# First layer by token halves, the second half a period behind it, and a rewritten prologue and first period

## The chip, the core and the metric

The kernel runs on one core of a Trainium2 chip. The metric is the device time of one execution in microseconds (us). Three runs of the kernel before gave 299.66 to 300.46, median 300.08.

## What is computed

For each of 8 batches ("blocks" below) and 8 heads, q, k and v are 576 x 64. Landmarks are means over 18 neighbouring tokens, 32 for q and 32 for k. Then

```
A  = softmax(q  @ k_lm.T / 8)      # 576 x 32
Bm = softmax(q_lm @ k_lm.T / 8)    # 32 x 32
C  = softmax(q_lm @ k.T / 8)       # 32 x 576
Z  = Bm.T / (norm1(Bm) * norminf(Bm) + 1e-6)
for _ in range(6): Z = 2 * Z - Z @ Bm @ Z
attn = A @ Z @ C @ v               # 576 x 64 per head
```

The heads are put side by side into x (4608 x 512), and two dense layers follow: h = x @ w_in (512 x 2048), g = h * sigmoid(h), out = g @ w_out (2048 x 512). Inputs and output are float32; the products run in bf16.

## The kernel before

Eight heads are held as two groups of four, with 4 x 32 landmark rows on the 128 partitions. x is never formed. The kernel folds Z, C, v and w_in into one matrix per block: z_mm gives zwT, and four m_units multiply it by w_in, 512 columns each, into mb (256 x 2048 as two halves of 128 rows). A unit is eight products of 64x32 tiles into two PSUM buffers, copied out by VectorE (L460) and ScalarE (L461). The first layer is then AT (A transposed, 256 x 576) against mb.

The program is written out by hand in the order in which each engine is to work. A prologue (L515 to L587) does all the attention of block 0. After it comes a loop of one "period" per block b, of 16 steps s. Step s of period b does one of the first layer's 16 slices of 128 columns for all 576 tokens (l1_mm, L469, four "hps" products into a two-bank PSUM tile; l1_act, L479, Silu by ScalarE into gT). Around it are laid the attention of block b + 1 and the second layer of block b - 1: l2_mm(n) (L489) issues the next n of its "ops" products. Sixteen ops fill one output tile of 128 tokens in the pool pso, which has one buffer; then ScalarE copies it to ost (L505) and SyncE stores it. An even block has four such tiles and an odd one five, since the 64 tokens left over of an even block are put at the front of the odd one (l1_tail, L484, on GpSimd). The lists EVEN and ODD (L510) say how many ops each step issues: 80 in an even period, 64 in an odd one. The tiles of block b are put into the queue at the end of period b (L733), so none is issued in period 0, and the five of block 7 follow the last period.

The attention of block b + 1, in order: landmarks (lmn; for blocks 0 and 1 by 18 "lmp" products per plane with the identity on TensorE, L151; for the others by GpSimd sums, L164); bdiag (L198) spreads their transposes into block-diagonal weights bd by four VectorE transposes of 32 partitions, and a fifth gives lmk; b_scores, b_max, b_exp, b_norm (Bm); f_mm, b_scale and f_out make the start of the iteration; six rounds of ns_mm and ns_step (L279 to L293) carry F = Z Bm and X as 128 + 32 columns ("fx"; the first 128 hold four heads' 32x32 blocks on the diagonal); c_scores, c_max, c_exp (C); c_transpose and c_out for blocks 0 and 1, a transposing DMA for the others; w_mm, w_out (C @ v); x_out, z_mm, z_out; a_scores in three parts, a_max, a_shift, a_exp, a_norm (A; the last product on GpSimd, L427), and AT by a_transpose and a_out (blocks 0 and 1) or by DMA.

In a period with d = 0 bdiag is in step 0, scores in 1 and 2, with the Exp table loaded for them and the Silu table after them (table, L119, a small ScalarE activation behind a table load), the rounds in steps 3 to 9, z_mm in 10 and the m_units in 11 to 14. In period 0, d = 4: steps 0 to 3 make the landmarks of block 1, the rest is four steps later, and three m_units of block 1 stand behind step 15 (L729). Loads go out from GpSimd's queue (load_qk, load_v, and the weights at L107 and L112). PSUM's eight banks are: psh, two tiles of two banks (hps and scp); pso, one; psa, three, for all else.

## Time and profile before

| | us |
|---|---|
| median of three runs | 300.08 |
| the profiled execution, its own time | 300.44 |
| its span in the profile | 298.7 |
| first hps product (end of the prologue) | 32.38 |
| first hps product of block 1 (end of period 0) | 65.94 |
| last run of ops products begins | 276.71 |
| PE busy in the span | 266.3 (89%) |

PE is TensorE's products, PEld its weight loads, DVE VectorE, ACT ScalarE, POOL GpSimd, SP SyncE. A row of the timeline has the start, the duration, the engine, the line of the program, the operation, what is written from what, and how many instructions are merged into it; a bracket gives the idle time before it and what ended that. Products overlap, so busy time is not a sum of separate times. PEclk in the slices is the granted TensorE clock in tenths.

### The profile page before, as it was taken

The page shows a single profiled execution, that of the slowest core. Times are in us where ns is not written, and L with a number is a line of the kernel's source. Part 1 is how long each engine was busy: PE and PEld are TensorE (multiplying, and loading weights), DVE is VectorE, ACT ScalarE, POOL GpSimd, SP SyncE. Part 2 cuts the span into 40 slices and gives each one's busy share as a digit, 9 for nine tenths or more (in the row PEclk, how much of TensorE's full clock was granted, in tenths as well). Part 3 has the DMA queues.
Part 4 walks back from the last instruction along what each step waited for, and adds up shares of the span by engine and source line. Part 5 has one row for each costly group of instructions (what it writes and reads, how often), then busy time and mean ns, then how long its engine had stood idle before and what let it go on. Part 6 is the DMA issues. An engine that isn't in the chain of part 4 may idle for free.

```text
span 298.7 us, 5888 instructions
## 1 busy us (share of the span) xinstructions
PE 266.3 (89%) x2305; PEld 150.7 (50%) x2340; DVE 165.8 (55%) x407; ACT 174.2 (58%) x337; POOL 118.2 (40%) x141
## 2 busy tenths in 40 slices
PE   1766886769999999999999999999999999999994
PEld 1543564525554555455645554465555554455441
DVE  4885689786668565746695567475757523000000
ACT  1225288356757874669567855686669556445211
POOL 7234321893199119740794079204940300100000
PEclk9999999787999999999999999999999999999999
DMA  6999999507673946629597939131903131110111
GB/s 111 208 211 207 207 210 202 70 15 134 115 102 90 188 95 96 130 44 183 100 148 114 170 40 151 46 79 53 175 35 72 34 97 37 38 68 35 72 70 70
DMA packets 36252, 32.30 MB, mean 108 GB/s; under 512 B 18816, under 2 KB 27008, under 8 KB 36224
## 3 DMA queue, kind: packets, MB, share of 16 engines
q0 software_dynamic: 13568, 18.35, 37.5%
q1 hardware_dynamic: 22656, 13.57, 20.0%
q8 instruction: 18, 0.29, 0.5%
q14 instruction: 10, 0.08, 0.1%
HBM read 36.70 MB, written 9.44 MB: 154 GB/s over the span
## 4 chain that ended last, share of the span: by engine, by line
PE 79%; DVE 9%; ACT 4%; issue 3%; DMA 2%; POOL 1%; ACTq 0%; POOLq 0%
PE ops L71 43%; PE hps L71 19%; PE sa L71 5%; PE mp L71 4%; ACT ost L505 3%; PE scp L71 2%; DMA nat<-in_q_dram 2%; DVE qkT L148 2%; PE fi L71 2%; PE wp L71 1%; PE lmp L71 1%; DVE cmx L306 1%; DVE arec L425 1%; DVE fx L289 1%; DVE fx L274 1%
## 5 line engine op out<-in xcount | busy, mean ns | idle before, releaser
L71 PE MATMUL ops<-w_out_sb,gT 128*128 128x512 bf16 x541 | 141.1, 382 | 5.3 <-ACT ost L505 2.0
L481 ACT ACTIVATE gT<-hps 128x576 bf16<-128x576 f32 x128 | 82.4, 651 | 69.0 <-PE hps L71 68.6
L71 PE MATMUL hps<-AT,mb 128*128 128x288 bf16 x512 | 85.3, 293 | 0.3 <-ACT gT L481 0.2
L71 PEld LDWEIGHTS <-gT 128*128 128x128 bf16 x576 | 52.2, 98 | 54.2 <-issue 11.3
L71 PEld LDWEIGHTS <-mb 128*128 128x128 bf16 x512 | 48.4, 100 | 25.8 <-issue 2.8
L427 POOL TENSOR_TENSOR an<-ex,arec 128x512 bf16<-128x512 bf16 (+1 forms) x24 | 21.4, 906 | 86.9 <-ACT gT L481 43.8
L148 DVE STREAM_TRANSPOSE qkT<-nat 128x576 f32<-128x576 f32 x32 | 39.7, 1240 | 1.6 <-DMA nat<-in_k_dram 1.2
L505 ACT COPY ost<-ops 128x512 f32<-128x512 f32 x36 | 21.1, 586 | 23.9 <-PE ops L71 22.1
L289 DVE SCALAR_TENSOR_TENSOR fx<-fx,fi 128x320 bf16<-128x320 bf16 (+1 forms) x48 | 20.7, 431 | 23.1 <-PE fi L71 23.0
L460 DVE CAST mb<-mp 128x512 bf16<-128x512 f32 x32 | 22.0, 688 | 14.4 <-PE mp L71 14.1
L170 POOL TENSOR_TENSOR lma<-nat 128x1152 f32<-128x1152 bf16 x12 | 28.6, 2380 | 0.0
L461 ACT CAST mb<-mp 128x512 bf16<-128x512 f32 x32 | 18.7, 583 | 4.6 <-PE mp L71 4.6
L121 ACT ACT_TABLE_LOAD x16 | 20.5, 1283 | 1.1 <-PEq L749 0.8
L71 PE MATMUL fi<-fx 128*128 128x160 bf16 (+1 forms) x96 | 14.9, 239 | 4.4 <-DVE fx L289 2.7
L71 PEld LDWEIGHTS <-fx 128*128 128x128 bf16 x96 | 8.7, 101 | 16.3 <-DVE fx L289 5.1
L71 PE MATMUL mp<-w_in_sb,zwT 64*32 64x512 bf16 x256 | 14.4, 407 | 2.7 <-ACT mb L461 1.5
L405 DVE TENSOR_REDUCE nm<-sa 128x16 bf16<-128x512 f32 (+1 forms) x24 | 13.7, 594 | 5.2 <-PE sa L71 5.0
L71 PEld LDWEIGHTS <-ident 128*128 128x128 bf16 x168 | 10.2, 120 | 11.8 <-issue 5.0
L418 ACT ACTIVATE ex<-sa 128x512 bf16<-128x512 f32 (+1 forms) x24 | 12.5, 526 | 5.7 <-PE sa L71 5.7
L314 ACT ACTIVATE eC<-scp,cbs 128x576 bf16<-128x576 f32 x16 | 11.7, 741 | 4.8 <-DVE cbs L309 4.7
L306 DVE TENSOR_REDUCE cmx<-scp 128x1 f32<-128x576 f32 x16 | 12.1, 755 | 4.0 <-PE scp L71 3.5
L71 PE MATMUL lmp<-nat,ident 128*128 128x64 bf16 x144 | 8.2, 229 | 6.7 <-DMA nat<-in_k_dram 5.6
(69 smaller groups left out, 247.9 us busy)
## 6 DMA issues: line engine op xcount, KB each, us to landing
out_dram<-ost SPq DMA_DIRECT2D x36, 256.0 KB, 2.2
nat<-in_k_dram POOLq DMA_DIRECT2D x16, 288.0 KB, 6.8
nat<-in_q_dram POOLq DMA_DIRECT2D x16, 288.0 KB, 8.3
v<-in_v_dram POOLq DMA_DIRECT2D x8, 576.0 KB, 7.0
w_in_sb<-in_moe_w_in_dram POOLq DMA_DIRECT2D x4, 512.0 KB, 13.4
w_out_sb<-in_moe_w_out_dram POOLq DMA_DIRECT2D x4, 512.0 KB, 16.2
AT<-an SPq DMA_TRANSPOSE x30, 4.3
eCT<-eC SPq DMA_TRANSPOSE x12, 3.7
```

What stands on the lines that cost most here:

```text
L71: nc.tensor.matmul(out=o, lhsT=lhsT, rhs=rhs, start=start, stop=stop, skip_group_check=True)
L121: nc.scalar.activation(out=spare[:, 1:2], in_=spare[:, 0:1], func=func)
L148: nc.vector.transpose(out=o.rearrange("p (l t) -> p t l", t=SEG), in_=nat_t[b][:, j, :].bitcast(FP).rearrange("p (t l) -> p t l", l=L))
L170: nc.gpsimd.tensor_tensor(out=a1, in0=nat[:, :, 0:3 * w], in1=nat[:, :, 3 * w:6 * w], op=OP.add)
L289: nc.vector.scalar_tensor_tensor(out=n[:, :, lo:160], in0=self.fx[:, :, lo:160], scalar=2.0, in1=self.p.rearrange("p (g n) -> p g n", g=2) ...
L306: nc.vector.tensor_reduce(out=mx, in_=self.s[g][:, :, 0:HF], op=OP.max, axis=AX.XY, negate=True)
L405: nc.vector.tensor_reduce(out=self.nm[0:pr, c:c + n, :], in_=self.sa[i][0:pr, 0:256 * n].rearrange("p (c h l) -> p c h l", h=8, l=L), op=O ...
L427: nc.gpsimd.tensor_tensor(out=self.an[0:pr, c:c + n, :].rearrange("p c (h l) -> p (c h) l", l=L), in0=x, in1=r.unsqueeze(2).to_broadcast(( ...
L460: nc.vector.tensor_copy(out=o[:, 0, :], in_=m[0])
L461: nc.scalar.copy(out=o[:, 1, :], in_=m[1])
L481: nc.scalar.activation(out=gT_t[b][:, dc, o:o + S].rearrange("p (a n) -> p a n", a=2), in_=h[:, :, 0:HF], func=AF.Silu)
L505: nc.scalar.copy(out=ost, in_=st["ps"])
```

## The change

1. The first layer's step s does two of the 128-column slices for one half of the tokens (288): steps 0 to 7 the first half, 8 to 15 the second. A step still has four hps products of 288 columns and one Silu.
2. The first two output tiles of a block enter the queue after step 7 of its own period, the others after step 15. The lists become CNT (periods 0 and 1), EVEN and ODD: 32, 64, then 76 and 68 in turn; 48 ops are left behind the last period.
3. For blocks 0 and 1 ("tiled") the 32x32 products (b_scores, f_mm, ns_mm) are done head by head on four diagonal 32x32 tiles of TensorE, eight products with 64 columns a round where there were two with 160; bdt isn't made. One VectorE transpose gives the landmarks (lmc), and four copies of 32 partitions (ScalarE in the prologue, GpSimd in period 0) fill bd.
4. sb, f0, the rounds' products and zt of every block share one bank, bb, of a new pool psn (one buffer), which the landmark sums also use. psa has two buffers in place of three. The third part of a_scores takes a two-bank tile of psh.
5. a_transpose and a_out work by token ranges (0 to 511, then 512 to 575) for both row halves, with the copy shared by VectorE and ScalarE.
6. The prologue and period 0 are reordered; d is 6 in period 0 and 4 in period 1. Block 2's landmarks are made on TensorE and its transposes on VectorE in steps 0 to 3 of period 1. The m_units that don't fit are done in the next period (units 1 to 3 of block 1 in steps 0 to 2 of period 1; of block 2 in steps 0 and 3 of period 2).
7. w_in is loaded by 512-column pieces, in another order with block 1's q, k and v and w_out; three loads stand between operations of the prologue.

In the diff "a" is the attention of the next block and "a0" that of the running one. self.tiled is b < 2; ns_mm and ns_step change in the same way as f_mm and f_out.

```diff
-    psa = ctx.enter_context(tc.tile_pool(name="psa", bufs=3, space=bass.MemoryType.PSUM))
+    psn = ctx.enter_context(tc.tile_pool(name="psn", bufs=1, space=bass.MemoryType.PSUM))
+    psa = ctx.enter_context(tc.tile_pool(name="psa", bufs=2, space=bass.MemoryType.PSUM))
...
+    def load_w_in(f):
+        nc.gpsimd.dma_start(
+            out=w_in_sb[:, :, 512 * f:512 * f + 512],
+            in_=moe_w_in.rearrange("(j p) n -> p j n", p=128)[:, :, 512 * f:512 * f + 512])
+
+    def load_w_out(j):
         nc.gpsimd.dma_start(
             out=w_out_sb[:, 4 * j:4 * j + 4, :],
             in_=moe_w_out[512 * j:512 * j + 512, :].rearrange("(c p) m -> p c m", p=128))
+
+    load_w_in(0)
+    load_w_in(1)
+    load_qk(1, (1, 0))
+    load_w_in(2)
+    load_qk(1, (3, 2))
+    load_w_in(3)
+    load_w_out(0)
+    load_w_out(1)
...
+        def lm_t(self, g):
+            nc.vector.transpose(
+                out=self.lmc[:, 2 * g:2 * g + 2].rearrange("p j l e -> p (j l e)").bitcast(FP),
+                in_=self.lmn[:, 2 * g:2 * g + 2, :].bitcast(FP))
+
+        def bd_expand(self, g, copy):
+            for h in range(4):
+                p = slice(32 * h, 32 * h + 32)
+                copy(out=self.bd[p, 2 * g:2 * g + 2, 32 * h:32 * h + 32, :],
+                     in_=self.lmc[p, 2 * g:2 * g + 2])
+
 
         def b_scores(self):
-            self.sb = ps1("sb")
+            self.bb = psn1("bb")
+            self.sb = self.bb[:, 448:512]
+            if self.tiled:
+                for g in range(2):
+                    for e in range(2):
+                        for h in range(4):
+                            p = slice(32 * h, 32 * h + 32)
+                            mm(self.sb[p, 32 * g:32 * g + 32], self.lmc[p, 2 * g, :, e],
+                               self.lmc[p, 2 * g + 1, :, e], start=(g == 0 and e == 0),
+                               stop=(e == 1))
+                return
...
+            if not self.tiled:
+                self.bdt = attp.tile([128, 2, 128], BF, tag="bdt", name="bdt", bufs=1)
+                self.expand(self.bdt, self.bmt)
 
         def f_mm(self):
-            self.f0 = ps1("f0")
+            w = self.fw = L if self.tiled else 128
+            self.f0 = self.bb[:, 0:2 * w].rearrange("p (g n) -> p g n", g=2)
             for g in range(2):
-                mm(self.f0[:, 128 * g:128 * g + 128], self.bdt[:, g, :], self.bdt[:, g, :],
-                   start=(g == 0), stop=True)
+                if self.tiled:
+                    for h in range(4):
+                        p = slice(32 * h, 32 * h + 32)
+                        mm(self.f0[p, g, :], self.bmt[p, g, :], self.bmt[p, g, :],
+                           start=(g == 0), stop=True)
+                else:
+                    mm(self.f0[:, g, :], self.bdt[:, g, :], self.bdt[:, g, :],
+                       start=(g == 0), stop=True)
 
...
         def f_out(self):
-            nc.vector.tensor_tensor(out=self.fx[:, :, 0:128],
-                                    in0=self.f0[:, 0:256].rearrange("p (g n) -> p g n", g=2),
-                                    in1=self.nrm.unsqueeze(2).to_broadcast((128, 2, 128)),
+            w = self.fw
+            nc.vector.tensor_tensor(out=self.fx[:, :, 0:w], in0=self.f0,
+                                    in1=self.nrm.unsqueeze(2).to_broadcast((128, 2, w)),
                                     op=OP.mult)
+            self.p = self.bb[:, 0:2 * (w + L)].rearrange("p (g n) -> p g n", g=2)
...
-            s = self.sa[i] = ps1("sa")
+            s = self.sa[i] = ps2("sa")[:, 0, :] if i == 2 else ps1("sa")
...
+        def a_transpose(self, k):
             if self.by_dma:
                 return
-            self.at = ps1("atp", BF)
-            for (c, (c0, c1)) in enumerate(TCH):
-                pr = c1 - c0
-                nc.tensor.transpose(self.at[:, c0:c1], self.an[0:pr, c, 128 * g:128 * g + 128],
-                                    ident[0:pr, 0:pr])
-
-        def a_out(self, g):
-            if not self.by_dma:
-                nc.vector.tensor_copy(out=self.AT[:, g, :], in_=self.at[:, 0:S])
+            self.at = (ps1("atp", BF) if self.b else
+                       pso.tile([128, 1024], BF, tag="o", name="atp"))
+            for r in range(2):
+                for c in ((0, 1, 2, 3), (4,))[k]:
+                    c0, c1 = TCH[c]
+                    o = 512 * r + c0 - 512 * k
+                    nc.tensor.transpose(self.at[:, o:o + c1 - c0],
+                                        self.an[0:c1 - c0, c, 128 * r:128 * r + 128],
+                                        ident[0:c1 - c0, 0:c1 - c0])
+
+        def a_out(self, k):
+            if self.by_dma:
+                return
+            iv = self.at.rearrange("p (r n) -> p r n", r=2)
+            if k == 0:
+                nc.vector.tensor_copy(out=self.AT[:, 0, 0:512], in_=iv[:, 0, :])
+                nc.scalar.copy(out=self.AT[:, 1, 0:512], in_=iv[:, 1, :])
+            else:
+                nc.vector.tensor_copy(out=self.AT[:, :, 512:S], in_=iv[:, :, 0:S - 512])
...
+    def l1_mm(b, s):
         h = ps2("hps")
-        for g in range(2):
-            for hf in range(2):
-                mm(h[:, hf, 0:HF], mb_t[b][:, g, 128 * dc:128 * dc + 128],
-                   AT_t[b][:, g, HF * hf:HF * hf + HF], start=(g == 0), stop=(g == 1))
+        hf, s = s // 8, s % 8
+        for i in range(2):
+            dc = 2 * s + i
+            for r in range(2):
+                mm(h[:, i, 0:HF], mb_t[b][:, r, 128 * dc:128 * dc + 128],
+                   AT_t[b][:, r, HF * hf:HF * hf + HF], start=(r == 0), stop=(r == 1))
         return h
 
-    def l1_act(b, dc, h):
-        o = (b % 2) * TL
-        nc.scalar.activation(out=gT_t[b][:, dc, o:o + S].rearrange("p (a n) -> p a n", a=2),
-                             in_=h[:, :, 0:HF], func=AF.Silu)
+    def l1_act(b, s, h):
+        o = (b % 2) * TL + HF * (s // 8)
+        s = s % 8
+        nc.scalar.activation(out=gT_t[b][:, 2 * s:2 * s + 2, o:o + HF], in_=h[:, :, 0:HF],
+                             func=AF.Silu)
...
-    EVEN = [4, 4, 8, 12, 4, 4, 4, 4, 4, 4, 4, 4, 4, 5, 5, 6]
-    ODD = [4, 4, 8, 8, 4, 4, 3, 3, 3, 3, 4, 3, 3, 3, 3, 4]
+    CNT = {0: [0] * 8 + [12, 4, 3, 3, 3, 3, 2, 2], 1: [2, 2, 2, 2, 2, 8, 10, 4] + [4] * 8}
+    EVEN = [4, 4, 8, 12, 4, 4, 4, 4] + [4] * 8
+    ODD = [4, 4, 8, 10, 2, 2, 3, 3] + [4] * 8
...
+    lp = psn1("lmp")
     for j in (1, 0):
         landmarks_pe(0, lp, j, 1)
         transpose_qk(0, j)
     landmarks_out(0, lp, 0, 2)
     a = Att(0)
     landmarks_pe(0, lp, 3, 1)
-    a.bdiag((0,))
+    a.lm_t(0)
+    a.bd_expand(0, nc.scalar.copy)
     transpose_qk(0, 3)
     landmarks_pe(0, lp, 2, 1)
+    transpose_qk(0, 2)
     landmarks_out(0, lp, 2, 2)
+    a.lm_t(1)
+    a.b_scores()
+    a.bd_expand(1, nc.scalar.copy)
+    a.b_max()
     a.c_scores(0)
-    a.bdiag((1,))
-    a.b_scores()
-    a.b_max()
-    a.c_max(0)
     a.b_exp()
-    a.c_exp(0)
-    a.c_scores(1)
+    a.a_start()
+    a.a_scores(0)
     a.b_norm()
     a.f_mm()
     a.b_scale()
     a.f_out()
     a.ns_mm()
-    a.c_transpose(0)
-    transpose_qk(0, 2)
+    a.c_max(0)
+    a.c_exp(0)
+    a.c_scores(1)
     a.ns_step()
     a.ns_mm()
-    a.a_start()
-    a.a_scores(0)
+    a.a_max(0)
+    a.a_shift(0)
+    a.a_exp(0)
+    a.ns_step()
+    a.ns_mm()
+    a.c_transpose(0)
     a.c_max(1)
     a.c_exp(1)
     a.c_out(0, nc.scalar.copy)
     a.ns_step()
     a.ns_mm()
     a.a_scores(1)
-    a.a_max(0)
-    a.a_shift(0)
-    a.a_exp(0)
+    a.a_norm(0)
+    load_w_out(2)
     a.ns_step()
     a.ns_mm()
-    a.c_transpose(1)
     a.a_max(1)
     a.a_shift(1)
+    a.a_exp(1)
+    a.c_transpose(1)
+    a.ns_step()
+    a.ns_mm(last=True)
     a.c_out(1, nc.scalar.copy)
-    a.a_exp(1)
-    a.ns_step()
-    a.ns_mm()
-    a.w_mm(0)
     a.a_scores(2)
     a.w_scale()
+    a.w_mm(0)
     a.w_out(0)
+    a.ns_step(last=True)
+    a.x_out()
+    a.a_norm(1)
+    load_v(1)
+    a.w_mm(1)
+    a.w_out(1)
+    a.z_mm()
     a.a_max(2)
     a.a_shift(2)
     a.a_exp(2)
-    a.ns_step()
-    a.ns_mm(last=True)
-    a.w_mm(1)
-    a.w_out(1)
     table(AF.Silu)
-    a.a_norm(0)
-    a.ns_step(last=True)
-    a.x_out()
-    a.z_mm()
-    a.a_norm(1)
     a.z_out()
+    a.a_transpose(0)
     a.m_unit(0)
+    a.a_out(0)
     a.a_norm(2)
-    load_qk(2)
-    a.a_transpose(0)
-    a.a_out(0)
-    a.a_transpose(1)
-    a.a_out(1)
+    load_w_out(3)
...
-        cnt = EVEN if b % 2 == 0 else ODD
+        cnt = CNT.get(b, EVEN if b % 2 == 0 else ODD)
         h = {}
         a0 = a
-        a = Att(b + 1) if nxt and b else None
-
-        d = 4 if b == 0 else 0
+        a = Att(b + 1) if nxt and b > 1 else None
+
+        d = (6, 4)[b] if b < 2 else 0
...
-            if b == 0 and s < 4:
+            if b < 2 and s < 4:
+
                 if s == 0:
-                    lp = pso.tile([128, 512], FP, tag="o", name="lmp")
-                l1(s)
-                act(s)
-                landmarks_pe(1, lp, ORD[s], 1)
-                transpose_qk(1, ORD[s])
+                    lp = psn1("lmp")
+                l1(s)
+                act(s)
+                landmarks_pe(b + 1, lp, ORD[s], 1)
+                transpose_qk(b + 1, ORD[s])
                 if s < 3:
                     a0.m_unit(s + 1)
-                else:
-                    landmarks_out(1, lp, 0, 4)
-                    a = Att(1)
+                if b == 0 and s == 0:
+                    a0.a_transpose(1)
+                    a0.a_out(1)
+                if s == 1 and b == 0:
+                    landmarks_out(b + 1, lp, 0, 2)
+                if s == 2 and b == 0:
+                    a = Att(b + 1)
+                    a.lm_t(0)
+                    a.bd_expand(0, nc.gpsimd.tensor_copy)
+                if s == 3:
+                    landmarks_out(b + 1, lp, 2 * (1 - b), 2 * (1 + b))
+                    a = a or Att(b + 1)
+                l2_mm(cnt[s])
+            elif b == 0 and s < 7:
+                l1(s)
+                act(s)
+                if s == 4:
+                    a.lm_t(1)
+                    a.bd_expand(1, nc.gpsimd.tensor_copy)
...
+                if b == 0:
+                    a.b_norm()
+                    a.f_mm()
+                    a.b_scale()
+                    a.f_out()
...
+            elif b == 0:
+                l1(s)
+                if s == 9:
+                    act(8)
+                    a.ns_mm()
+                    a.c_transpose(0)
+                    a.a_norm(0)
+                    a.ns_step()
+                    a.c_out(0)
+                elif s == 10:
+                    a.ns_mm()
+                    a.c_transpose(1)
+                    a.w_scale()
+                    a.ns_step()
+                    a.ns_mm()
+                    a.c_out(1)
+                    a.a_norm(1)
+                elif s == 11:
+                    a.w_mm(0)
+                    a.ns_step()
+                    a.ns_mm()
+                    a.w_out(0)
+                    a.a_norm(2)
+                elif s == 12:
+                    a.w_mm(1)
+                    a.ns_step()
+                    a.ns_mm()
+                    a.w_out(1)
+                    a.ns_step()
+                elif s == 13:
+                    a.ns_mm(last=True)
+                    a.ns_step(last=True)
+                    a.x_out()
+                    a.a_transpose(0)
+                    a.a_out(0)
+                elif s == 14:
+                    a.z_mm()
+                    a.z_out()
+                    a.a_transpose(1)
+                    a.a_out(1)
+                else:
+                    a.m_unit(0)
+                act(s)
+                l2_mm(cnt[s])
...
             if s == 0 and b % 2:
                 l1_tail(b)
-            if s == 1 and b + 3 < B:
+            if b > 1 and s in (0, 3):
+                while a0.m_done < (3 if s == 0 else 4):
+                    a0.m_unit(a0.m_done)
+            if b == 0 and s == 0:
+                load_qk(2)
+            if s == (4 if b < 2 else 1) and b + 3 < B:
                 load_qk(b + 3)
             if s == 7 + d // 2 and b + 2 < B:
                 load_v(b + 2)
-            if s in (8 + d // 2, 10 + d // 2) and b + 2 < B:
-                landmarks_pool(b + 2, s - 8 - d // 2)
-            if b + 2 < B and 9 + d // 2 <= s <= 12 + d // 2:
-                transpose_qk(b + 2, ORD[s - 9 - d // 2])
-        if b == 0:
-            for f in range(1, 4):
-                a.m_unit(f)
-        n = 4 + b % 2
-        l2_state["queue"] += [(b, 128 * i) for i in range(n)]
+            if b and b + 2 < B:
+                if s in (8 + d // 2, 10 + d // 2):
+                    landmarks_pool(b + 2, s - 8 - d // 2)
+                if 9 + d // 2 <= s <= 12 + d // 2:
+                    transpose_qk(b + 2, ORD[s - 9 - d // 2])
+            if s in (7, 15):
+                n = 4 + b % 2
+                l2_state["queue"] += [(b, 128 * i) for i in ((0, 1) if s == 7 else range(2, n))]
```

## The prediction

> **What bounds the kernel now.** I read the forty slices of the page first, then a table of stretches, then the timeline where two stretches differ.
>
> ```profile
> PE   1766886769999999999999999999999999999994
> PEclk9999999787999999999999999999999999999999
> DMA  6999999507673946629597939131903131110111
> ...
> L71 PE MATMUL ops<-w_out_sb,gT 128*128 128x512 bf16 x541 | 141.1, 382 | 5.3 <-ACT ost L505 2.0
> ```
>
> PE is full from the tenth slice on (7.5 us each) and has holes before it. PEclk dips only in slices 8 to 10. The table of stretches (columns: stretch, its length, busy PE, PEld, DVE, ACT, POOL with counts, clock, DMA share, GB/s) puts sizes to it:
>
> ```profile
> 0.00:30.00 30.00, 16.64 (x197) 11.85 (x197) 20.03 (x60) 9.90 (x22) 13.92 (x25) 1.00 1.02 185
> 30.00:60.00 30.00, 23.05 (x283) 15.95 (x282) 23.86 (x55) 17.85 (x36) 12.45 (x16) 0.94 1.00 172
> 60.00:75.00 15.00, 12.07 (x94) 6.14 (x95) 10.54 (x24) 8.96 (x20) 9.68 (x13) 0.77 0.43 75
> 90.00:120.00 30.00, 29.27 (x261) 16.28 (x264) 19.10 (x47) 20.88 (x42) 16.24 (x19) 1.00 0.67 118
> ```
>
> From 90 us on PE lacks 0.7 us in 30: only fewer or faster products shorten that part, and any wait put into it is paid in full. Before 66 us a chain sets the time: the first hps product starts at 32.38 (end of prologue), the first of block 1 at 65.94 (end of period 0), the first of block 2 near 97.45. The last ops run is 276.71 to 295.0: 80 products at 0.2155 each. I price by start-to-start times, since busy time counts overlap: ops 0.2155 us, four hps 0.49, 18 lmp 0.62, an mp unit 0.34.
>
> The total of products is nearly unchanged. So the question is how many holes the change fills, and how many it makes.
>
> **The prologue (32.38 to 28.5, -3.9).** The chain of block 0 runs from the last landmark copy (11.23) through sb, exp, f, six fx rounds, zt (27.72), mp (28.75) and AT (32.95). One transpose for lmc (0.25, as lmk) takes the place of four into bd and one lmk (0.98 + 0.21); bd is filled beside it by four copies on ACT, at most 0.27 each (the lmn cast). Without bdt (0.29) and with f_out at 64 instead of 256 columns (about 0.22, the 128x64 row, for 0.42), fx rounds begin near 15.5 instead of 16.70. A tiled product is not in the trace. Its bounds: 24 wp products took 0.51 together cold, so eight are at least 0.17; eight one after the other, each with a weight load of 0.13 (the cold fx load) and a product of 0.062 (lmp, 1.12 / 18), are 1.5 at most; I take 0.35, nearer to wp, whose tiles are also 32 columns wide. The fx step has 128 columns: between 0.21 (64) and 0.47 (320), I take 0.28. Each round saves 0.2, six 1.2. The rest is order: a_norm(0) comes before the fourth step, not after all six, so zt falls at about 24.6. Then ACT has an exp (0.4), the table load with its dummy (1.5), mb (0.59) and half of AT (0.59): 25.3 to 28.5. AT is late there, no longer the POOL pair 27.41 to 29.73. At the upper bound, 1.15 more in each of six rounds, the start would be near 35.4, and period 0 about 7 later too; at the lower one, 27.4.
>
> POOL's order matters: in the trace its tenth load starts at 7.45, when the second has landed at 7.2, and so on, always eight behind. The fifteenth load (w_out 1) then goes out when the seventh (w_in 1) lands, about 18, since 512 KB take 2.45 us; a_norm(0) behind it is due at 19.9. Unit 0 needs w_in 0 alone, there at 15.5. The last piece of w_out lands near 42, before the ops of step 9 want it. These edits cost nothing; with that cover gone each is worth one landing, 2.45.
>
> **Period 0 (33.56 to 30.4, -3.2).** Steps 0 to 3 stay: cold PE, 2.7 us for the first, and DVE's four transposes of 1.25 and three mb casts of 0.69; the half a_transpose adds 0.3. bd goes to POOL, four copies, 0.10 (memset) to 0.46 (128x128) each, 0.4 taken; b_scores doesn't wait for them. Against this, table(Exp) now stands behind eight Silu, not six: b_exp is 1.3 later (two at 0.65) than the 11.0 us after period start of before. The tail of the chain is then packed: steps 9 to 15 hold 7 hps groups (3.4), 20 ops (4.3), fx, ctp, wp, atp, zt, mp (3.3), about 12 us with small waits, where before fx to zt and four mp units took 49.4 to 65.9. So it ends at 28.5 + 30.4 = 58.9, with 32 ops done that were not. Bounds of this term: -5.5, if ACT's queue doesn't hold the chain, to +3, if it does twice.
>
> **Period 1 (31.5 to 33.6, +2.1).** Same 64 ops. Added: 72 lmp products, 4 x 0.62 = 2.5 on PE, and four transposes on DVE in steps 0 to 3, so bd is ready 0.7 late. Gone: the cold stretch, hps groups of 1.0 and ops of 0.43 between 65.9 and 72, some 3 us; PE's packed end of period 0 is the reason why I expect it warm. A new wait: the list 2, 2, 2, 2, 2, 8 ends an output tile six products into step 5. pso has one buffer, so the next ops waits for the ost copy, and on ACT that stands behind Silu, table load and b_exp: (0.65 + 1.5 + 0.65 + 0.6) less 1.9 of PE work and 0.2 lead = 1.7 net.
>
> **Periods 2 to 7 and the end (201.25 to 203.2, +1.9).** Gain: 48 instead of 80 ops behind the last hps, 32 x 0.2155 = -6.9. Given back: three mp units of block 2 move in (+1.0), two of them back to back on two psa buffers (0.69 + 0.1, +0.8). sa(2) now sits in an hps buffer, so the second hps of step 3 waits for its exp. In period 3 these are the rows to look at:
>
> ```profile
> 138.09 0.29 PE L71 MATMUL sa<-nm,ident 64*64 64x256 bf16 x1
> ...
> 138.31 1.15 PE L71 MATMUL hps<-AT,mb 128*128 128x288 bf16 x8
> 138.52 0.59 ACT L505 COPY ost<-ops 128x512 f32<-128x512 f32 x1 [0.16 <-PE sa L71]
> ...
> 139.00 0.38 ACT L418 ACTIVATE ex<-sa 64x256 bf16<-64x256 f32 x1
> ...
> 139.40 1.28 ACT L121 ACT_TABLE_LOAD   x1
> ...
> 140.80 1.17 ACT L481 ACTIVATE gT<-hps 128x576 bf16<-128x576 f32 x2
> ```
>
> The exp ends at 139.38, the second hps group would start at 138.8: 0.38 in even periods, three times (+1.1). The larger toll is in the odd ones. Even counts sum to 76 of 80, so an odd period starts with 4 left over, and 4 + 4 + 8 leave twelve of the next tile done: the boundary falls four ops into step 3. Its ost copy is behind the table load and two Silu. Without the copy at 138.52, exp is 138.4 to 138.8, table to 140.3, Silu to 141.45, ost to 142.05; PE has come to the boundary at 140.2. So 1.9 us, and 0.6 more where steps 4 and 5 have 2 ops, not 4, and the fx step waits behind two a_norm on DVE: 2.5 in periods 3 and 5 (+5.0). Period 7 has no table load: 0.8. Sum -6.9 + 1.0 + 0.8 + 1.1 + 5.0 + 0.8 = +1.8, and 0.1 for rounding.
>
> **Sum.** -3.9 - 3.2 + 2.1 + 1.9 = -3.1 on the profiled 300.44 (span 298.7, 1.74 around it): 297.3. That run stands 0.36 above the median 300.08, so 297.0.
>
> [...]
>
> **Rivals.**
> A, as summed: 297.0, from 294 to 299.2; 0.46.
> B, the ost waits aren't there, because ACT comes to the copies earlier than I read: -3.1 - 1.7 - 5.0 - 0.8 = -10.6, 289.5; or the front gives 3 more. For it: ACT is busy 58%. Against: ACT works in order, and the table load stands ahead. Below 294: 0.18.
> C, slower: ACT's queue in period 0 (eight Silu, table load, exps, before any fx round) holds the chain so that block 1 starts no earlier than before. Then only +2.1 + 1.9 = +4.0 is left, 304. It decides from a block 1 start later than 62.8 (58.9 + 3.1 + 0.9). For it: chains on four engines rarely run as packed as on paper; against: 4 us of margin. 0.22 for everything above 301.
> D, the change doesn't do what it says: time only moves from the end to the front, block 1 near 62: within 0.3% (0.9 us, about what a measurement of this kernel can tell from no change): 0.14.
>
> Faster is A and B: 0.64; same 0.14; slower 0.22. The range leaves out the far half of B and of C: 291.0 to 303.0.
>
> **What would show it.** First hps at 28.5; first hps of block 1 at 58.9; lmp in period 1 with clock 1.0; 48 ops behind the last hps, 10.3 us; ops waiting for ost about 1.9 us once in periods 3 and 5 and 1.7 in period 1. A first hps after 31, a tiled round over 0.7, or a clock under 0.9 in period 1 would make the number wrong; no ost waits over 1 us would too, to the fast side.

## The result and the profile after

The changed kernel took 301.31 us (median of 20 runs, 298.77 to 302.5), the kernel before, run beside it, 299.89 (20 runs, 298.72 to 301.35). The ratio is 1.0043, with a 95% interval of 1.0026 to 1.0061: slower, by 0.4%, where 297.0 and faster was forecast. 301.31 lies inside the stated range, 291.0 to 303.0, but on the side that the forecast gave 0.22. The profiled execution of the changed kernel took 302.18, its span is 300.4.

The slices and the ops group of the changed kernel's page, to be set against those of before:

```profile
PE   1777979998998799999799999997899999989994
PEclk9999999999999799999999999999999999999999
DMA  6999999717765932819394828303480513011011
...
L72 PE MATMUL ops<-w_out_sb,gT 128*128 128x512 bf16 x538 | 142.6, 382 | 9.6 <-ACT ost L580 6.2
```

Most holes of slices 2 to 9 are smaller and the dip of PEclk in slices 8 to 10 is gone. There is a new dip in slice 14 (98 to 105 us), and the ops group now waits 6.2 us for ost, where it waited 2.0. The same stretches of the changed kernel (columns as before):

```profile
0.00:30.00 30.00, 18.36 (x264) 12.62 (x265) 19.18 (x55) 12.92 (x32) 14.82 (x26) 1.00 1.06 179
30.00:60.00 30.00, 28.16 (x371) 17.06 (x372) 17.67 (x49) 19.23 (x40) 10.53 (x21) 1.00 1.09 190
60.00:75.00 15.00, 13.28 (x168) 8.78 (x171) 11.28 (x20) 10.81 (x23) 3.23 (x5) 1.00 0.44 82
...
90.00:120.00 30.00, 26.48 (x229) 13.86 (x231) 17.30 (x45) 17.65 (x36) 14.27 (x17) 0.94 0.52 97
```

Up to 75 us PE does 8 us more than before; from 90 to 120 it does 2.8 us less, at a clock of 0.94. Set period by period (time from a block's first hps to the next block's):

| stretch | before | forecast | after | after less forecast |
|---|---|---|---|---|
| prologue | 32.38 | 28.5 | 28.46 | 0.0 |
| period 0 | 33.56 | 30.4 | 32.00 | +1.6 |
| period 1 | 31.51 | 33.6 | 33.48 | -0.1 |
| period 2 | 32.78 | 34.1 | 38.41 | +4.3 |
| periods 3 and 5, each | 29.29 | 32.65 | 32.16 | -0.5 |
| periods 4 and 6, each | 32.78 | 32.3 | 32.25 | 0.0 |
| period 7 and the end | 44.33 | 39.2 | 39.22 | 0.0 |

The terms of the last five rows are those of the forecast's sum, spread over the periods (an even period has 4 ops fewer than before, 0.86, an odd one 4 more). Added up, 1.6 - 0.1 + 4.3 - 1.0 = 4.8, which is 302.18 less the forecast for the profiled execution, 297.3. One period holds nearly all of it. This is period 2 of the changed kernel, from its timeline:

```profile
91.31 2.37 POOL L186 TENSOR_TENSOR lma<-nat 128x1152 f32<-128x1152 bf16 x1
...
95.77 0.41 PE L72 MATMUL mp<-w_in_sb,zwT 64*32 64x512 bf16 x8
...
96.45 0.45 POOL L194 TENSOR_TENSOR lmn<-lmd,lmc 128x128 bf16<-128x128 f32 x1
...
96.92 0.37 PE L72 MATMUL mp<-w_in_sb,zwT 64*32 64x512 bf16 x1 [0.73 <-ACT mb L532]
...
96.93 1.25 DVE L225 STREAM_TRANSPOSE bd<-lmn 32x128 f32<-32x128 f32 x4 [3.04 <-POOL lmn L194]
...
98.37 0.65 DVE L531 CAST mb<-mp 128x512 bf16<-128x512 f32 x1
...
99.07 0.41 PE L72 MATMUL mp<-w_in_sb,zwT 64*32 64x512 bf16 x7 [1.78 <-DVE mb L531]
...
101.06 1.91 PE L72 MATMUL ops<-w_out_sb,gT 128*128 128x512 bf16 x4
```

and its clock (the number before the last two) in the table of stretches:

```profile
98.00:104.00 6.00, 4.93 (x36) 2.80 (x36) 3.30 (x9) 3.99 (x10) 1.02 (x2) 0.72 1.03 177
```

Read it from the bottom: four ops take 1.91, where four warm ones (at a granted clock of 1.00) take 1.02, since the clock is at 0.50 there (100 to 103 us). The mp product ahead of them waited 1.78 for a cast of mb on VectorE. That cast had its input at 96.2, but stands behind the four bd transposes in VectorE's order, and these waited 3.04 for GpSimd's last landmark sum. The sum is late because GpSimd's queue starts later; the rows of its timeline before, in period 1, are

```profile
81.20 2.71 POOL L427 TENSOR_TENSOR an<-ex,arec 128x512 bf16<-128x512 bf16 x3 [11.05 <-DVE wsc L337]
...
95.43 0.46 POOL L178 TENSOR_TENSOR lmn<-lmd,lmc 128x128 bf16<-128x128 f32 x1
```

and the first of them in the changed kernel is

```profile
82.22 2.71 POOL L486 TENSOR_TENSOR an<-ex,arec 128x512 bf16<-128x512 bf16 x3 [11.80 <-DVE wsc L397]
```

From the first a_norm to the last sum GpSimd works without a gap, 14.7 us in both. Before, a_norm began 15.3 us into a period of 31.5, and the sums ended 1.6 us ahead of period 2. With d = 4 it begins 21.8 us into a period of 33.5, and 21.8 + 14.7 = 36.5 is 3.0 too late.

### The profile page after: what moved, and what is told of

It is laid out like the page before. It is cut to its first block, busy times and chain, and to the rows that moved or that the text cites. A ratio compares the mean times of both kernels' runs of the same rounds, so it can differ in the third digit from the quotient of the medians.

```text
span 300.4 us, 6240 instructions
## 1 busy us (share of the span) xinstructions
PE 267.7 (89%) x2482; PEld 150.6 (50%) x2520; DVE 160.4 (53%) x394; ACT 177.5 (59%) x349; POOL 110.7 (37%) x139
## 4 chain that ended last, share of the span: by engine, by line
PE 71%; DVE 9%; ACT 8%; POOL 6%; issue 3%; DMA 3%; ACTq 0%; POOLq 0%
PE ops L72 37%; PE hps L72 16%; PE sa L72 5%; PE mp L72 4%; ACT ost L580 3%; PE bb L72 3%; DMA nat<-in_q_dram 3%; PE scp L72 3%; PE lmp L72 2%; DVE arec L484 2%; POOL lma L186 2%; ACT gT L556 1%; POOL an L486 1%; DVE fx L350 1%; ACT ex L477 1%
## 5 line engine op out<-in xcount | busy, mean ns | idle before, releaser
L72 PE MATMUL ops<-w_out_sb,gT 128*128 128x512 bf16 x538 | 142.6, 382 | 9.6 <-ACT ost L580 6.2
L72 PEld LDWEIGHTS <-gT 128*128 128x128 bf16 x576 | 51.4, 98 | 57.5 <-issue 16.6
L350 DVE SCALAR_TENSOR_TENSOR fx<-fx,bb 128x320 bf16<-128x320 bf16 (+2 forms) x48 | 18.5, 386 | 27.5 <-PE bb L72 27.4
L186 POOL TENSOR_TENSOR lma<-nat 128x1152 f32<-128x1152 bf16 x10 | 23.8, 2379 | 0.0
L72 PEld LDWEIGHTS <-ident 128*128 128x128 bf16 (+1 forms) x240 | 12.8, 113 | 13.5 <-issue 5.1
L72 PE MATMUL lmp<-nat,ident 128*128 128x64 bf16 x216 | 10.9, 217 | 7.5 <-DMA nat<-in_k_dram 6.6
L72 PE MATMUL bb<-fx 32*32 32x64 bf16 (+2 forms) x168 | 13.4, 215 | 2.8 <-DVE fx L328 1.6
L72 PEld LDWEIGHTS <-fx 32*32 32x32 bf16 (+1 forms) x168 | 8.2, 96 | 14.6 <-DVE fx L350 4.6
```

The source lines that it names most:

```text
L72: nc.tensor.matmul(out=o, lhsT=lhsT, rhs=rhs, start=start, stop=stop, skip_group_check=True)
L186: nc.gpsimd.tensor_tensor(out=a1, in0=nat[:, :, 0:3 * w], in1=nat[:, :, 3 * w:6 * w], op=OP.add)
L350: nc.vector.scalar_tensor_tensor(out=n[:, :, lo:], in0=self.fx[:, :, lo:], scalar=2.0, in1=self.p[:, :, lo:], op0=OP.mult, op1=OP.subtract)
```

## The experiments

Each run is the changed kernel with the edit shown; ratios are to the kernel before. Theory: the excess is at period 2, from GpSimd's late sums through bd and the casts. The front of the profile varies between executions of the same instructions (the first hps at 26.4 to 28.5), so profiles are compared period by period.

**e1, sums earlier.** The sums of block 3 at steps 4 and 6 of period 1.

```diff
-                if s in (8 + d // 2, 10 + d // 2):
-                    landmarks_pool(b + 2, s - 8 - d // 2)
+                p0 = 4 if b == 1 else 8
+                if s in (p0, p0 + 2):
+                    landmarks_pool(b + 2, s - p0)
```

> The GpSimd landmark sums of block 3 are issued in steps 4 and 6 of period 1 instead of 10 and 12; nothing else moves. Theory (the sums end at 96.9, bdiag waits 3.0 us for them on VectorE, the mb casts of the units of block 2 stand behind bdiag, TensorE idles 2.5 us and its clock falls to 0.72 for 98 to 104 us): the sums then end near 82, period 2 falls from 38.4 to about 34, the clock there is 1.00, and the time is 297.0 (-4.3 on 301.3). Rival (the loss in period 2 is two units back to back on two PSUM buffers): period 2 stays above 37.5 and the time is 300.5 to 301.3.

Measured: 300.52, ratio 1.0014 (0.9994 to 1.0034). The wait for the sums is gone and period 2 takes 34.72, not 38.41, as the theory said. But period 1 takes 36.75 for 33.48 and gives it back, at a place that no term had, so the rival's time was met without its reason. VectorE's timeline of this run, and a stretch behind it:

```profile
68.54 0.22 DVE L267 TENSOR_REDUCE bmx<-bb 128x2 f32<-128x64 f32 x1 [0.36 <-PE bb L72]
68.80 2.92 DVE L270 TENSOR_SCALAR bbs<-bmx 128x2 f32<-128x2 f32 x1
```

```profile
74.00:76.00 2.00, 2.00 (x19) 1.82 (x18) 1.38 (x3) 0.37 (x1) 1.92 (x3) 0.50 1.16 239
```

That operation on two elements takes 0.17 in the changed kernel. It ends at 71.72, and GpSimd's addition lma (69.28, 2.40) ends at 71.68. It starts 0.48 ahead of that addition, while GpSimd issues a DMA; what held it there isn't shown. b_exp waits 1.57 for it, the ost copy is behind b_exp, and ops waits 2.67 for ost in place of 0.98. After that wait the clock is at half for some 3 us, an estimate of 1.5 of the remaining 1.6.

**e2, units first.** In step 0 of period 2, m_units 1 and 2 are issued ahead of bdiag.

```diff
                 l1(s)
+                if b == 2:
+                    a0.m_unit(1)
+                    a0.m_unit(2)
                 a.bdiag()
```

> In step 0 of period 2 units 1 and 2 of block 2 are issued ahead of bdiag, so their casts stand before it on VectorE; the landmark sums stay late. Theory (lateness of the sums is the cause, the order only chooses who waits): the wait between the two units shrinks to the 0.8 us of the casts, but the score products of block 3 still can't start before the sums (96.9) and bdiag (1.5), 98.4, against 99.98 now: at most 1.6 gained, 299.7 to 301, with a clock still below 1.00 in part. Rival (the order on VectorE is the whole cause): as good as moving the sums, 297.

Measured: 297.98, ratio 0.9937 (0.9913 to 0.9962). TensorE's timeline of this run, in period 2:

```profile
94.46 0.48 PE L72 MATMUL mp<-w_in_sb,zwT 64*32 64x512 bf16 x8 [0.73 <-ACT mb L532]
...
97.27 0.25 PE L72 MATMUL bb<-lmk,bd 128*128 128x32 bf16 x4 [0.87 <-DVE lmk L230]
```

Its larger waits there are 0.73 for the second unit and 0.87 for lmk, the clock stays at 1.0, and period 2 takes 35.38 for 38.41. So the rival was nearer: the sums are still late, and most of their cost came from what stood behind bdiag.

**e3, counts.** No tile ends between the table load and the ost copy.

```diff
-    EVEN = [4, 4, 8, 12, 4, 4, 4, 4] + [4] * 8
-    ODD = [4, 4, 8, 10, 2, 2, 3, 3] + [4] * 8
+    EVEN = [4, 4, 8, 12, 4, 4, 4, 4] + [4] * 5 + [5, 5, 6]
+    ODD = [4, 4, 8, 8, 2, 2, 2, 2] + [4] * 8
```

> Only the lists of periods 2 to 7 change: even 80 ops (the last three steps 5, 5, 6), odd 4, 4, 8, 8, 2, 2, 2, 2 and eight times 4, so every output tile ends where a step's ops end. Theory (a tile that ends inside step 3 waits for an ost copy behind the table load and two Silu): the waits of 1.56 at 143.64 and 208.06 and of 0.72 in period 7 go, 0.2 of normal boundary waits come back, the time is 297.9 (-3.4). Rival (the ost wait only stands where TensorE would wait for the first-layer Silu or fx anyway): under -1, 300.5.

Measured: 300.58, ratio 1.0027 (1.0006 to 1.0048), the rival's figure and a miss for the theory: the three ost waits (1.56, 1.56, 0.72) are gone, but the fx wait of 0.54 stays with steps of 2 ops, 0.3 comes back where a tile now ends, and an odd and an even period together fall only from 64.4 to 63.8. What takes back the rest isn't traced.

**e5, without tiles.** self.tiled is False for all blocks, with bdiag and bdt back; the new order stays.

```diff
-            self.tiled = b < 2
+            self.tiled = False
...
-    a.lm_t(0)
-    a.bd_expand(0, nc.scalar.copy)
+    a.bdiag((0,))
...
-                    a.lm_t(1)
-                    a.bd_expand(1, nc.gpsimd.tensor_copy)
+                    a.bdiag((1,))
```

> The diagonal tiles are undone for blocks 0 and 1: bdiag on VectorE, lmk, bdt and 128-wide products return; the order of everything stays. Theory (a tiled product of eight costs 0.22 us and its fx step 0.29, against 0.45 and 0.47 cold): the first hps product comes 2 to 3 us later than 28.46, the first of block 1 another 0 to 1 later, and the time is 303.5 to 305. [...]

Measured: 300.99, ratio 1.0034 (1.0012 to 1.0056). By the median (300.99, the changed kernel's 301.31) the diagonal tiles bring nothing. First hps at 27.76, though a product of a round takes 0.45 for 0.29 and its fx step 0.48 for 0.29. In this profile TensorE was warm from about 21 to 28 (the mp unit ahead of the first hps took 0.41), in that of the changed kernel cold to 35 (0.63 for that unit, 0.41 for the one at 35.80); from the last 18 lmp products (9.99 here, 10.90 there, 10.21 in e7, which is tiled and was warm there too) to the first hps it took 17.77 here, 17.56 in the changed kernel and 16.23 in e7. With the clock alike the tiles are worth 1.5 in these two profiles, 16.23 against 17.77. Of the eleven profiles with this tiled prologue nine take 17.56 or 17.57, e10 17.02 and e7 16.23, so an untiled prologue may run warm more often; that is not tested, and why the medians are equal stays open.

**e6, other counts.** 72 ops in every period.

```diff
+    EVEN = [4, 4, 8, 12, 4, 4, 4, 4] + [4] * 6 + [2, 2]
+    ODD = [4, 4, 8, 8, 4, 4, 4, 4] + [4] * 8
```

> Only the two count lists change: 72 products in every period (even 4, 4, 8, 12, then 4, the last two steps 2; odd 4, 4, 8, 8, then 4), so that each output tile ends at the end of a step and no tile ends between the table load and the Silu, while steps 4 and 5 keep 4 products. Theory (the copy behind the table load costs 1.56, and thin steps 4 and 5 cost 0.54 at the fx step): b_scores of period 3 to that of period 5 falls from 64.41 to about 62.4, and the whole from 301.3 to about 296.5. Rival (the boundary wait of 0.32 and the 0.35 of the second hps stay, as they did with the list that ended the tile elsewhere): 63.2, whole about 298.5. In either case the stall at the start of period 2 stays.

Measured: 297.78, ratio 0.9943 (0.9923 to 0.9964). An odd and an even period together take 62.76, between the two figures: ost and fx waits are gone, 0.35 stays at one tile's end.

**e8, the shift first.** In period 0 the second shift of the scores goes ahead of f_mm.

```diff
                     a.b_norm()
+                l2_mm(2)
+                a.a_shift(1)
+                a.a_exp(1)
+                if b == 0:
                     a.f_mm()
                     a.b_scale()
                     a.f_out()
-                l2_mm(2)
-                a.a_shift(1)
-                a.a_exp(1)
```

> In period 0 the second shift product of the scores is issued ahead of the first f product, no longer behind it: TensorE's 1.12 us wait for bmt then holds neither that shift nor the exp behind it. Theory (that wait is what made block 1 start 1.6 later than forecast): first hps of block 1 from 60.46 minus 28.46 = 32.0 to about 30.9 after the first hps, and the whole 301.3 to 300.2. Rival (TensorE has enough other products queued in steps 9 to 15 that the start of block 1 is set by their number): no change, within 0.3.

Measured: 300.01, ratio 1.0006 (0.9977 to 1.0036), too wide to tell by time. In the profile the wait for bmt falls from 1.12 to 0.36, and b_scores of block 1 to the first hps of block 1 goes from 20.78 to 20.13. So 0.65 of period 0's 1.6 is this, short of the theory's 1.1; the whole period is 30.50 in that profile, but the rest of the difference lies in its first steps, where the clock varies (the second run of 18 lmp products takes 0.69 here and 1.16 in the changed kernel).

**e9, sums two steps earlier.** They are issued at steps 8 and 10.

```diff
-                if s in (8 + d // 2, 10 + d // 2):
-                    landmarks_pool(b + 2, s - 8 - d // 2)
+                if s in (8, 10):
+                    landmarks_pool(b + 2, s - 8)
```

> The GpSimd landmark sums of block 3 are issued at steps 8 and 10 of period 1, not 10 and 12, and not at 4 and 6 as in the earlier run. Theory (these sums are late by some 3 us and hold the block diagonals and the mb casts behind them; the earlier run gave that back because the sums then ran beside the small operations of the scores): the wait of the block diagonals for lmn is gone, period 2 falls by 3.5 to 4, the whole to about 297.5. Rival (beside the fx rounds the sums slow VectorE as much as beside the scores): over 299.5, with VectorE's fx steps at 1 us and more.

Measured: 301.82, ratio 1.0075 (1.005 to 1.0101), and bd still waits 3.09. The rival's time came, but not its reason: VectorE's fx steps keep their 0.49. GpSimd's timeline of this run:

```profile
81.08 2.15 POOL L486 TENSOR_TENSOR an<-ex,arec 128x512 bf16<-128x512 bf16 x2 [11.79 <-DVE wsc L397]
83.19 2.36 POOL L186 TENSOR_TENSOR lma<-nat 128x1152 f32<-128x1152 bf16 x1
...
88.73 0.66 POOL L486 TENSOR_TENSOR an<-ex,arec 64x256 bf16<-64x256 bf16 x1
...
95.35 0.45 POOL L194 TENSOR_TENSOR lmn<-lmd,lmc 128x128 bf16<-128x128 f32 x1
```

The sums come behind the same a_norm as before, which waits for wsc, and the work is only arranged otherwise: 81.08 to 95.80 is 14.7 us again. The point at which they are issued is not the cause: the queue is full from a_norm on, and only what is put ahead of a_norm ends earlier. Period 2 takes 39.64 here, for 38.41, with nearly the same waits (0.73 and 1.83): the clock is at 0.60 over 6 us, from 96 to 102.

**e11, sums split.** One half at step 1 of period 1, where GpSimd is idle, the other at step 10; nothing else.

```diff
-                if s in (8 + d // 2, 10 + d // 2):
-                    landmarks_pool(b + 2, s - 8 - d // 2)
+                if b > 1 and s in (8, 10):
+                    landmarks_pool(b + 2, s - 8)
+                if b == 1 and s in (1, 10):
+                    landmarks_pool(3, 0 if s == 1 else 2)
```

> The changed kernel with that split of the GpSimd sums alone (steps 1 and 10 of period 1), all else as it was, the mp units of block 2 behind the block diagonals too. Theory (GpSimd's queue is the cause at period 2): lmn is there before period 2, the wait of 3.04 is gone, period 2 goes from 38.41 to about 34.5, the whole from 301.3 to about 297.5. Rival (sums beside the transposes of period 1 delay VectorE there, or the back to back units cost the same without them): over 299.5.

Measured: 297.03, ratio 0.992 (0.9894 to 0.9945). VectorE's and then TensorE's timeline of this run, where period 2 begins:

```profile
92.92 0.69 DVE L531 CAST mb<-mp 128x512 bf16<-128x512 f32 x1 [0.34 <-PE mp L72]
93.53 1.24 DVE L225 STREAM_TRANSPOSE bd<-lmn 32x128 f32<-32x128 f32 x4
```

```profile
95.50 0.41 PE L72 MATMUL mp<-w_in_sb,zwT 64*32 64x512 bf16 x8
96.64 0.48 PE L72 MATMUL mp<-w_in_sb,zwT 64*32 64x512 bf16 x8 [0.73 <-ACT mb L532]
...
98.16 1.02 PE L72 MATMUL ops<-w_out_sb,gT 128*128 128x512 bf16 x4
```

bd waits for nothing, the second unit has no second wait, four ops take 1.02. The 0.73 that is left is that unit's, back to back on two buffers, which the forecast had at 0.8. Both forecasts of the theory came, 34.71 for 34.5 in period 2 and 297.03 for 297.5. This one edit is worth 3.7 us in period 2 (38.41 to 34.71), 3.7 by the ratios to the kernel before, and 4.3 in the medians (301.31 to 297.03), whose two sets of runs have the kernel before at 299.89 and 299.46.

**e12, e1 with bbs in two operations.** To e1 is added

```diff
-            nc.vector.tensor_scalar(out=self.bbs, in0=bmx, scalar1=s2, scalar2=None, op0=OP.mult)
+            for g in range(2):
+                nc.vector.tensor_scalar(out=self.bbs[:, g:g + 1], in0=bmx[:, g:g + 1], scalar1=s2,
+                                        scalar2=None, op0=OP.mult)
```

> The earlier run with the sums of block 3 at steps 4 and 6 of period 1, with one edit more: the scaling of the negated maxima to bbs is done as two operations on one element per partition instead of one on two. [...] Rival (any small VectorE operation waits for GpSimd's addition, whatever its shape): still near 2.9, and the whole as in that run, 300.5.

Measured: 298.44, ratio 0.9958 (0.9937 to 0.998). VectorE's timeline of this run, with lma on GpSimd from 69.46 to 71.86 and from 75.04 to 77.40:

```profile
68.98 0.21 DVE L271 TENSOR_SCALAR bbs<-bmx 128x1 f32<-128x1 f32 x2
...
70.03 0.15 DVE L371 TENSOR_SCALAR cbs<-cmx 128x1 f32<-128x1 f32 x1
...
75.50 1.99 DVE L293 TENSOR_TENSOR bm<-pb,brec 128x64 bf16<-128x64 f32 x1
```

Two operations on one element take 0.21 together, at the place where one on two elements took 2.92. They end before the addition starts, so they weren't beside it; cbs was, and takes 0.15, so it is not every small operation that waits. The ops wait is 0.99, for 2.67 in e1. bm, which reads two tensors from SBUF, still waits: 1.99 for 0.22, about to the end of the second addition; the first product of the rounds behind it waits 1.54, where the changed kernel waits 0.52. Period 1 is 34.33 for e11's 33.48, which is the larger part of the 1.4 by which this run's median is above e11's.

**e7 and e10, together.** m_unit 1 of block 2 ahead of bdiag and units 2 and 3 at steps 1 and 3 of period 2; e6's counts; e8's order; 6, 12 in place of 8, 10 in the list of period 1. In e7 the sums are issued as in e9, in e10 as in e11. What is not shown above already:

```diff
+                if b == 2:
+                    a0.m_unit(1)
                 a.bdiag()
...
-            if b > 1 and s in (0, 3):
-                while a0.m_done < (3 if s == 0 else 4):
-                    a0.m_unit(a0.m_done)
+            if b == 2 and s in (1, 3):
+                a0.m_unit(a0.m_done)
```

> Five edits together: mp unit 1 of block 2 ahead of the block diagonals, units 2 and 3 at steps 1 and 3; the GpSimd sums of block 3 at steps 8 and 10 of period 1; 72 products in every period; the first tile of period 1 ends at the end of step 5; in period 0 the second shift of the scores ahead of the first f product. Theory (each removed wait is paid in full): -3.3 -0.5 at period 2, -4.5 for the counts, -1.0 in period 1, -1.1 in period 0, so about 291. Rival (what is freed at one place is waited for at the next, as with the earlier sums): not under 295.

> As the kernel with all five edits, but the GpSimd sums of block 3 are split: the first half at step 1 of period 1, where GpSimd stands idle from the copy of the tail (57.26 there) to the loads of block 4 (64.54), the second half at step 10. Theory (what holds the block diagonals in period 2 is GpSimd's own queue, which runs back to back for 15 us from the first a_norm of period 1, so only work taken out of that stretch makes them early): the sums end near 86.5 instead of 92.05, the wait of 2.14 for lmk goes, TensorE's clock stays at 1.0 in period 2, and the whole falls from 292.75 to about 290. Rival (the wait at lmk is made by the order on VectorE and not by GpSimd): no change, within 0.5.

Measured: e7 292.75, ratio 0.9774 (0.9754 to 0.9794); e10 292.12, ratio 0.9736 (0.9703 to 0.9769). Both beat both kernels, by over 2%. e7 is nearer to its theory (291) than to its rival (295); e10 missed its 290. e10's edge over e7 in the medians, 0.6, is within their spread, and the front of its profile is later (first hps at 27.50, e7's at 26.44). But from the scores of block 2 to those of block 4 it takes 59.19 for 61.81. TensorE's wait for lmk is 0.78 for 2.14, and the clock with it; the same stretch of e7 and then of e10:

```profile
95.00:100.00 5.00, 4.95 (x39) 2.63 (x37) 3.24 (x7) 2.39 (x8) 0.00 (x0) 0.69 1.15 211
```

```profile
95.00:100.00 5.00, 4.88 (x45) 2.59 (x44) 4.08 (x9) 4.11 (x12) 0.00 (x0) 1.00 1.23 209
```

PE counts as busy for 4.9 of 5 us in both, with 39 instructions and 45.

## Why the prediction was wrong

**The step that failed** is the line "three mp units of block 2 move in (+1.0), two of them back to back on two psa buffers (0.69 + 0.1, +0.8)". It counts the units on TensorE and their PSUM buffers. It leaves out that their casts stand behind bdiag on VectorE, and that bdiag waits for GpSimd, whose a_norm moves with d = 4. The 0.8 itself is right (0.73 in e11). The missing cost is 3.7 of period 2's 4.3 us: with the sums out of the way (e11) the period takes 34.71, for 34.1 forecast. The other 0.6 stays open. That e11's 297.03 is the forecast's 297.0 is luck in part, since +1.6 in period 0 and this 0.6 stand against the -1.0 of periods 3 and 5. The late sums could be read from before: 14.7 us of gapless GpSimd work with 1.6 us to spare, and an a_norm that moves from 15.3 into the period to some four steps later. The prediction asked about GpSimd's order for the prologue's loads and not for this.

**Period 0, +1.6.** By the forecast the rounds start at about 46.9 (58.9 less 12 for steps 9 to 15); they started at 48.49. The 12 us were right (48.49 to 60.46). 0.65 of the delay is the shift product held behind f_mm (e8). The rest lies ahead of b_exp, which was to start 12.3 into the period (11.0 and 1.3) and starts at 13.40 here. In e7, with the same instructions up to there, it starts at 12.38; there 18 lmp products take 0.69 from about 30 us on, here from about 35 (1.17 and 1.16 before). So the rest goes with the clock, by comparison of profiles and not by an experiment.

**The prologue, 28.5**, was met (28.46), but not by the terms given, and so closely by luck: the eleven profiles of this prologue have it from 26.44 to 28.46. The fx step (0.29) and the tiled product (0.29 for eight, where 0.35 was taken) were about right, and yet without tiles the median is the same (e5). By the medians the order carries the gain; the tiles' share, 1.5 in two profiles with like clock (1.2 and some was said), is about as large as what the clock does there, 1.3. Cold, the eight products of a round take 0.29; warm, in period 0, 0.24, with the next products begun 0.16 after the first (48.49 and 48.65).

**Period 1** was right in its sum: the clock is 1.00 from 60 to 75, lmp takes 0.62, start to start. Its terms were not: the ost wait is 0.98, not 1.7 (what is written for it, 3.4 less 1.9 and 0.2, makes 1.3), the fx start waits 0.52, which no term of this period had, TensorE doesn't wait for bd, and 2.5 + 0.7 - 3 + 1.7 is 1.9, not 2.1.

**The waits of periods 3, 5 and 7** came where they were forecast, behind the table load and two Silu. This is the changed kernel in period 3:

```profile
140.54 1.28 ACT L137 ACT_TABLE_LOAD   x1
...
141.94 1.17 ACT L556 ACTIVATE gT<-hps 128x576 bf16<-128x576 f32 x2
143.00 0.59 ACT L580 COPY ost<-ops 128x512 f32<-128x512 f32 x1
143.64 0.59 PE L72 MATMUL ops<-w_out_sb,gT 128*128 128x512 bf16 x2 [1.56 <-ACT ost L580]
...
148.25 0.31 PE L72 MATMUL bb<-fx 128*128 128x160 bf16 x2 [0.53 <-DVE fx L350]
```

1.56 where 1.9 was said, 0.53 where 0.6 was, 0.72 for 0.8 in period 7; e6 takes them away. In even periods the second hps group of step 3 comes 0.84 after the first, 0.35 more than 0.49, where 0.38 was said, though the rows given for it, 139.38 less 138.8, make 0.58. So rival B, that the ost waits aren't there, falls, and so does C: block 1 started at 60.46, not after 62.8 (58.9 + 3.1 + 0.9 is 62.9). The forecast had the right shape for slower, a chain held in one engine's queue, and looked for it in ACT's queue of period 0.

## What to carry to other kernels

When a chain is moved later in a repeated stage, take every engine that carries part of it and add up: where its first piece now starts, plus the gapless work behind it, against the end of the stage; moving an issue point inside a full queue changed nothing (e9: bd waits 3.09 for 3.04). When work is moved into another stage, look in each engine's order at what now stands ahead of its last step, a cast or a copy, not only at the product: issuing two units ahead of a waiting transpose took 3.0 us off the period (e2), where early sums took 3.7. Waits of 1.78 to 2.67 us in a full TensorE cost more than themselves here, since the clock after them was 0.50 to 0.72 (the changed kernel, e1, e7, e9); after those of 1.56 in periods 3 and 5 it stayed at 1.00.

## What the runs showed of the hardware

**The clock.** Waits of 0.73 to 0.87 us at period 2 left the granted clock at 1.00 (e2, e10, e11), and so did those of 1.56 in periods 3 and 5 of the changed kernel; after one of 2.14 it was 0.69 over the next 5 us (e7), after one of 2.67 0.50 from 74 to 76 us (e1), after 0.73 and 1.78 in short order 0.72 over 6 us (the changed kernel), with 0.50 from 100 to 103. In the prologue the same instructions ran warm or cold: the mp unit ahead of the first hps took 0.41 in e7 and 0.63 in the changed kernel, and the way from the last lmp products to that hps 16.23 and 17.56. The stretch 0 to 30 us of the changed kernel prints a clock of 1.00 all the same, so there the state is read from the lengths of the products: in e10, which took 0.63 for that unit too, the clock prints 0.50 from 26 to 32 us.

**VectorE beside GpSimd.** A VectorE operation from SBUF to SBUF on two elements took 2.92 in e1 (0.17 in the changed kernel), one with two SBUF inputs 1.99 in e12 (0.22 in period 3 of the changed kernel), each about up to the end of GpSimd's addition (71.72 and 71.68, 77.49 and 77.40). Others took their usual time beside such an addition: a cast from PSUM 0.69 (the changed kernel, at 93.20), the one-element cbs 0.15 (e1 and e12). What in an operation makes the difference isn't shown, and neither is what held e1's operation in the 0.48 ahead of the addition.
